# Linear attention, mixture of experts and a second network on one core: two maxima taken in another way

## The chip, the core and the metric

The kernel runs on 1 core of a Trainium2 chip. The metric is the device time of one execution in microseconds (us). Engines are named as the profile names them: PE (matrix products; PEld is its weight load), DVE (VectorE), ACT (ScalarE), POOL (GpSimd) and SP (SyncE, which only issues transfers here). Each engine takes its instructions in program order; an instruction waits for the semaphores of those it needs.

## The reference

Three parts follow each other. The first is attention without a softmax over pairs of tokens: q is normalised over its 64 features, k over the tokens.

```
q_s = exp(q - max(q, axis=-1));  q_s = q_s / (sum(q_s, axis=-1) + 1e-9)
k_s = exp(k - max(k, axis=2));   k_s = k_s / (sum(k_s, axis=2) + 1e-9)
kv  = einsum('bhsd,bhse->bhde', k_s, v)
out = einsum('bhsd,bhde->bhse', q_s, kv)
```

There are 8 batches, 8 heads, 576 tokens and 64 features, in float32. The second part sends each token to one of 8 experts (512 to 1024 to 512, ReLU); the third is `max(x@w1, x@w2, x@w3) @ w_out` (512 to 768 to 512).

## The kernel before

A **unit** is half of a batch's heads, so there are 16 units, n = 0 to 15, n = 2 * batch + half. A unit's q and k lie in SBUF as tiles of 128 partitions by 4 heads by 5 rows by 64 features: each partition holds five rows (tokens) of each head. The steps of a unit are small functions: `k_max` (maximum over the five rows, on DVE), `k_tr` (PE turns it, DVE finishes the maximum and puts it on a diagonal, L238 and L241), `k_exp` (PE spreads it into PSUM, the matmul at L248; DVE subtracts, L251; ACT takes the exponential, L253), `q_max` (maximum over 64 features for 20 rows, DVE L221), `q_exp` (DVE subtracts the row's maximum, L228; ACT takes one exponential over 1280 elements, L229; for unit 1 POOL subtracts), `q_sum` and `q_norm` (DVE, L259 to L268), `kv_mm`, `kv_norm`, then for each of two pairs of heads `q_tr` (PE turns q, ACT copies it rounded, L327, or L324 in the first two batches), `q_lo` (DVE subtracts the rounded copy to get the rest, L335), `x_mm` (PE, L353), `x_lo` (DVE L371) and `logit_mm`.

Beside this, PE works through the experts' products in **slots**. One slot is a group of 12 products of 128x288 (L611 for the first layer, L629 for the second), and 32 slots make a batch. Each result leaves PSUM through ACT and DVE in the first layer (L616, L617), and through ACT (L634, first half) or DVE (L636, second half) in the second; four PSUM buffers serve them. Experts' weights are split into a rounded part (ACT L588) and a rest (POOL L595). Pieces of the last network's weights are turned from float64 to float32 meanwhile (ACT L682 and L684, DVE L677 to L694, POOL L685, L686 and L695). POOL also issues indirect transfers for the router (L489).

The order is fixed by tables of slots. `STEADY` gives, for units 4 to 15, the slot of each step counted from the unit's START (16 slots apart). So the front steps of unit n+1 are written in between the back steps of unit n: the second pair of heads of unit n has `q_tr` in its slot 15, `q_lo` in 16 and `x_mm` in 17, and `q_max` and `k_max` of unit n+1 stand at slot 12, its `q_exp` at 15, its `k_tr` at 16. Within a slot the group of products comes first, then the steps of the older unit. Units 2 and 3 have their own table (`EARLY`); units 0 and 1 and the front of unit 2 run before the first expert product, in the order of the list `first`. This is the start, about 50 us long, in which PE has little to do. Below, a **second-half place** is the stretch in which an even unit's slots 12 to 17 meet the second layer of the second half (evictions by DVE L636); there are six of them, about 70 us apart. At the six places of odd units evictions go through ACT L634.

Of the kernel before, what the change touches and what calls it, by code (L numbers as in the profile page):

```python
# [9 lines left out]
F32 = mybir.dt.float32  # L10
# [3 lines left out]
ACTF = mybir.ActivationFunctionType  # L14
# [20 lines left out]

# batches whose attention output comes from plain float32 products instead of three with split operands
NFULL = 2

# The order of the work beside the experts' matrix products, in slots of one group of 12 products; a unit is
# half of a batch's heads. STEADY: slots after a unit's START for the steps in FRONT, and those in BACK for  # L40
# each pair of heads; EARLY: the same for the first units, from the first slot on. LOAD: a unit's loads.
# ROUTE: the router's steps after START of a batch's second unit, for batch 0 and 1 from the first slot on.
# DEC: pieces of the float64 weights, after START of even units, of odd units and of the last one.
STEADY = ((-4, -1, -4, 0, 1, 3, 6, 6, 7, 8), (10, 10, 13, 14, 15), (15, 16, 17, 18, 19))
EARLY = {
# [11 lines left out]
def tile_linear_attention__then__moe(  # L57
# [21 lines left out]

# [1 line left out]
    const = ctx.enter_context(tc.tile_pool(name="const", bufs=1))  # L81
# [24 lines left out]

# [1 line left out]
    es_moe = ExitStack()  # L108
# [20 lines left out]

# [1 line left out]
    def setup():  # L131
# [40 lines left out]

# [1 line left out]
    units = {}  # L174
# [35 lines left out]
    def k_max(b, hb):  # L210
        u = units[b, hb]
        u["mx"] = sm.tile([128, 4, D], F32, tag="kmx", name="kmx")
        vec.tensor_reduce(
            out=u["mx"], in_=u["k"].rearrange("p h c d -> p h d c"), axis=AX.X, op=ALU.max
        )

    def q_max(b, hb):
        u = units[b, hb]
        qt = u["q"].rearrange("p h c d -> p (h c) d")
        m = sm.tile([128, 20, 1], F32, tag="qm", name="qm")  # L220
        vec.tensor_reduce(out=m[:, :, 0], in_=qt, axis=AX.X, op=ALU.max)  # L221
        u["qm"] = m

    def q_exp(b, hb):
        u = units[b, hb]
        qt = u["q"].rearrange("p h c d -> p (h c) d")
        eng = nc.gpsimd if (b, hb) == (0, 1) else vec
        eng.tensor_tensor(out=qt, in0=qt, in1=u["qm"].to_broadcast([128, 20, D]), op=ALU.subtract)  # L228
        act(out=qt, in_=qt, func=ACTF.Exp)  # L229

# [141 lines left out]

    # the logits with tokens as columns: column tile c of the array takes tokens 128 c on; the last 64 follow on tile 0
    def logit_mm(b, hb, pr):
# [17 lines left out]

# [1 line left out]
    def route_1(b):  # L394
# [60 lines left out]
    def route_4(b):  # L455
# [22 lines left out]
        )  # L478
        # the position of a token that leaves its batch's majority expert; BIG for the others
        pool.tensor_scalar(out=a, in0=a, scalar1=-float(BIG), scalar2=None, op0=ALU.add)  # L480
# [12 lines left out]

# [1 line left out]
    events = {}  # L495
# [27 lines left out]
    for n, s0 in START.items():  # L523
        b, hb = divmod(n, 2)
        if n in EARLY:
            t, s0 = EARLY[n], 0
        else:
            t = STEADY
        if n > 2:
            at(LOAD.get(n, START.get(n - 2, 0) + 9), load_unit, b, hb)  # L530
        for d, f in zip(t[0], FRONT):
            if d is not None:
                at(s0 + d, f, b, hb)
        for pr in range(2):
            for d, f in zip(t[1 + pr], BACK):
                at(s0 + d, f, b, hb, pr)
        if hb == 1:
            s0 = START[n]
            r1, r2 = (s0 + ROUTE[0], s0 + ROUTE[1]) if n > 3 else ROUTE1
            at(r1, logit_tr, b)  # L540
            at(r1, route_1, b)
            at(r2, route_2, b)
            at(r2 + 3, route_3, b)
            at(r2 + 4, route_4, b)
            for c in range(5):
                at(r2 + 5 + 2 * c, route_5, b, c)
# [4 lines left out]

# [1 line left out]
    raw_t = {}  # L553
# [98 lines left out]

# [1 line left out]
    dec = deque((i, j) for j in range(8) for i in range(4))  # L654
# [12 lines left out]
    def dec_bits():  # L667
        if not dec_r:
            return
        i, j, raw = dec_r.popleft()  # L670
        lo, hi = raw[:, :, 0], raw[:, :, 1]
        f = dc_p.tile([128, 384], I32, tag="df", name="df")
        p = dc_p.tile([128, 384], I32, tag="dp", name="dp")
        a2 = dc_p.tile([128, 384], F32, tag="da", name="da")
        r = dc_p.tile([128, 384], F32, tag="dr", bufs=2, name="dr")
        # sign, exponent less 896 and the upper 20 bits of the mantissa
        vec.tensor_scalar(out=f, in0=hi, scalar1=0x07FFFFFF, scalar2=3,  # L677
                          op0=ALU.bitwise_and, op1=ALU.logical_shift_left)
        vec.scalar_tensor_tensor(out=f, in0=hi, scalar=-0x40000000, in1=f,
                                 op0=ALU.bitwise_and, op1=ALU.bitwise_or)  # L680
        vec.tensor_scalar(out=p, in0=f, scalar1=-0x00800000, scalar2=None, op0=ALU.bitwise_and)
        act(out=a2, in_=hi.bitcast(F32), func=ACTF.Abs)  # L682
        # the lower 32 bits, added with one rounding
        act(out=r, in_=lo.bitcast(U32), func=ACTF.Copy, scale=2.0 ** -52)  # L684
        nc.gpsimd.tensor_tensor(out=r, in0=r, in1=p.bitcast(F32), op=ALU.mult)  # L685
        nc.gpsimd.tensor_tensor(out=r, in0=r, in1=f.bitcast(F32), op=ALU.add)  # L686
        dec_m.append((i, j, a2, r))

    def dec_store():
        if not dec_m:  # L690
            return
        i, j, a2, r = dec_m.popleft()
        # under float32's range, by the upper word (0x38100000 and on, read as a float): zero
        vec.tensor_scalar(out=a2, in0=a2, scalar1=1.125 * 2.0 ** -15, scalar2=None, op0=ALU.is_ge)  # L694
        nc.gpsimd.tensor_tensor(out=r, in0=a2, in1=r, op=ALU.mult)  # L695
        dma(out=w32_d[i][:, j], in_=r)
# [7 lines left out]

# [1 line left out]
    m_all = [t.rearrange("p j n -> (p j n)").rearrange("(k f) -> k f", f=F2) for t in w32_d[0:3]]  # L706
# [29 lines left out]

    # ================= program =================
    with tc.manual_schedule():
# [95 lines left out]

# [1 line left out]
        sl = {}  # L836

        def fx_table():
# [43 lines left out]
            vec.tensor_reduce(out=sf[:, 0:4], in_=pr, axis=AX.X, op=ALU.add)  # L882
            # start = valid * (start0 + SLOT * j)
            vec.tensor_scalar(out=sf[:, 4:5], in0=jc, scalar1=float(SLOT), scalar2=None, op0=ALU.mult)
            vec.scalar_tensor_tensor(
                out=sf[:, 2:3], in0=sf[:, 4:5], scalar=sf[:, 3:4], in1=sf[:, 2:3], op0=ALU.mult, op1=ALU.add
            )
            # static start = min(start + CAP * (1 - valid), CAP)
            vec.tensor_scalar(
# [3 lines left out]
            vec.tensor_scalar(out=sf[:, 3:4], in0=sf[:, 4:5], scalar1=float(CAP), scalar2=None, op0=ALU.min)  # L893
            # trips of the general loop: 0 where the static slots cover everything
            nsl = incl[:, w - 1:w]
# [55 lines left out]

        # half a piece of a minority expert's weights: 256 rows of 512 columns
        def fx_w(e_reg, i):
# [33 lines left out]

        # the tokens' upper and lower parts side by side: the first pass multiplies both with the
        # weights' upper part, the second the upper part with the weights' lower part
        def fx_mm(ps, x, ws, kh):  # L990
# [9 lines left out]

        # adds the two parts and turns tokens to columns
        def fx_sum(raw):
# [62 lines left out]

        # steps between the groups of the second network; one that leaves its sum open in PSUM comes
        # only where the next step follows before that bank is needed again
        fix = deque((f, False) for f in (fx_table, fx_gather, fx_soft, lambda: None, fx_tr))
# [12 lines left out]

        # chunks: (sources of y, N, list of (scale, writer))
        def chunk_l2(c, hs, part=0):
# [20 lines left out]

        # chunk B holds the last 64 tokens of each batch, in two parts; the second carries the packed tokens
        order = [(c, 0) for c in range(B)] + [(B, 0), (B, 1)]
# [113 lines left out]
```

## Time and profile before

| what | us |
|---|---|
| median of 3 runs | 1250.62 |
| runs, lowest to highest | 1249.36 to 1254.8 |
| profiled execution: span from first to last instruction | 1248.6 |
| PE busy in the span | 1193.2 (96%) |
| DVE busy | 647.8 (52%) |
| ACT busy | 447.0 (36%) |
| POOL busy | 380.4 (30%) |

Only the span of the profiled execution is on the page; its whole time is not listed beside it. It lies 0.8 us under the fastest run and 2.0 us under the median, so whatever lies around the span is small. "Busy" is the share in which an engine had an instruction in flight. An idle time has a releaser: the instruction whose semaphore came last. The granted clock of PE is 1.00 at 2.4 GHz and 0.50 at 1.2 GHz.

### The profile page before, as it was taken

The page shows a single profiled execution, that of the slowest core. Times are in us where ns is not written, and L with a number is a line of the kernel's source. Part 1 is how long each engine was busy: PE and PEld are TensorE (multiplying, and loading weights), DVE is VectorE, ACT ScalarE, POOL GpSimd, SP SyncE. Part 2 cuts the span into 40 slices and gives each one's busy share as a digit, 9 for nine tenths or more (in the row PEclk, how much of TensorE's full clock was granted, in tenths as well). Part 3 has the DMA queues.
Part 4 walks back from the last instruction along what each step waited for, and adds up shares of the span by engine and source line. Part 5 has one row for each costly group of instructions (what it writes and reads, how often), then busy time and mean ns, then how long its engine had stood idle before and what let it go on. Part 6 is the DMA issues. An engine that isn't in the chain of part 4 may idle for free. (4 is left out here: it accounts for less than half of the span.)

```text
span 1248.6 us, 19283 instructions
## 1 busy us (share of the span) xinstructions
PE 1193.2 (96%) x7518; PEld 1054.4 (84%) x7518; DVE 647.8 (52%) x1161; ACT 447.0 (36%) x864; POOL 380.4 (30%) x466
## 2 busy tenths in 40 slices
PE   4699999999999999999999999999999999999996
PEld 3598998989899898999888888888888888888995
DVE  7779787787878789534442414132331313232211
ACT  2463554546454554534331223122232213221211
POOL 1257767676776667772002000000000000000000
PEclk9799999999999999999999999999999999999998
DMA  6776555675665544353512121211222111210001
GB/s 167 183 198 175 166 176 159 175 214 148 202 202 164 170 128 148 123 188 99 169 35 79 36 67 52 83 44 34 85 68 76 46 56 51 51 51 1 35 17 24
DMA packets 141455, 135.68 MB, mean 109 GB/s; under 512 B 70045, under 2 KB 104637, under 8 KB 140336
## 3 DMA queue, kind: packets, MB, share of 16 engines
q1 hardware_dynamic: 139648, 134.01, 36.1%
q8 instruction: 61, 1.00, 0.3%
q0 software_dynamic: 1712, 0.39, 0.2%
q14 instruction: 34, 0.28, 0.1%
HBM read 106.99 MB, written 27.62 MB: 108 GB/s over the span
## 5 line engine op out<-in xcount | busy, mean ns | idle before, releaser
L813 PE MATMUL pm<-yh,wf 128*128 128x512 f32 (+2 forms) x2160 | 464.8, 375 | 0.0
L813 PEld LDWEIGHTS pm<-yh,wf 128*128 128x128 f32 x2160 | 385.9, 188 | 72.5
L629 PE MATMUL yp<-h,w 128*128 128x288 f32 x1536 | 226.3, 303 | 0.2 <-DVE h L617 0.2
L611 PE MATMUL hp<-xs,w 128*128 128x288 f32 x1536 | 218.9, 299 | 0.0
L629 PEld LDWEIGHTS yp<-h,w 128*128 128x128 f32 x1536 | 212.1, 192 | 3.6 <-DVE h L617 0.5
L611 PEld LDWEIGHTS hp<-xs,w 128*128 128x128 f32 x1536 | 208.1, 190 | 2.8 <-POOL w L595 0.2
L595 POOL TENSOR_TENSOR w<-stg,w 128x512 fp32r<-128x512 f32 x126 | 179.4, 1427 | 77.0 <-ACT w L588 74.9
L820 DVE TENSOR_TENSOR tm<-tm,pm 128x512 f32<-128x512 f32 (+2 forms) x60 | 38.6, 643 | 256.6 <-ACT tm L819 152.3
L1077 POOL DMA_INDIRECT out_dram<-oc,ftb x1 | 1.0, 983 | 548.4 <-ACTq L1149 548.4
L831 PE MATMUL op<-wo,hc 128*128 128x512 f32 (+1 forms) x666 | 152.8, 390 | 0.0
L831 PEld LDWEIGHTS op<-wo,hc 128*128 128x128 f32 (+1 forms) x666 | 124.5, 187 | 26.3
L819 ACT ACTIVATE tm<-pm 128x512 f32<-128x512 f32 (+2 forms) x60 | 33.7, 562 | 230.9 <-PE pm L813 230.2
L617 DVE SCALAR_TENSOR_TENSOR h<-hp,h 128x288 fp32r<-128x288 f32 x128 | 56.6, 451 | 58.8 <-ACT h L616 58.5
L616 ACT ACTIVATE h<-hp 128x288 fp32r<-128x288 f32 x128 | 52.2, 408 | 84.6 <-PE hp L611 84.2
L588 ACT ACTIVATE w<-stg 128x512 fp32r<-128x512 f32 x128 | 78.8, 621 | 0.0
L823 ACT ACTIVATE hc<-tm 128x512 fp32r<-128x512 f32 (+2 forms) x60 | 35.8, 597 | 93.9 <-DVE tm L821 93.9
L824 DVE TENSOR_TENSOR hc<-tm,hc 128x512 fp32r<-128x512 f32 (+2 forms) x60 | 38.9, 649 | 39.8 <-ACT hc L823 39.8
L833 ACT ACTIVATE oc<-op,tsrc 128x512 f32<-128x512 f32 x32 | 22.1, 689 | 101.9 <-PE op L831 101.9
L489 POOL DMA_INDIRECT tab_d<-tsrc,rpi x40 | 45.9, 1147 | 37.5 <-DMA tab_d<-tsrc,rpi 26.2
L685 POOL TENSOR_TENSOR dr<-dr,dp 128x384 f32<-128x384 f32 x32 | 32.5, 1015 | 53.2 <-ACT h L616 37.3
L228 DVE TENSOR_TENSOR q<-q,qm 128x1280 f32<-128x1280 f32 x15 | 42.7, 2849 | 0.0
L821 DVE TENSOR_TENSOR tm<-tm,pm 128x512 f32<-128x512 f32 (+2 forms) x60 | 38.6, 644 | 7.0 <-DVE tm L820 0.9
(219 smaller groups left out, 1179.1 us busy)
## 6 DMA issues: line engine op xcount, KB each, us to landing
stg<-in_moe_w_dram SPq DMA_DIRECT2D x31, 1024.0 KB, 5.7
fw<-in_moe_w_dram SPq DMA_DIRECT2D x24, 512.0 KB, 3.8
v<-in_v_dram SPq DMA_DIRECT2D x80, 128.0 KB, 4.8
draw<-in_moe_w_dram SPq DMA_DIRECT2D x24, 384.0 KB, 4.1
y_d<-y SPq DMA_DIRECT2D x32, 288.0 KB, 2.7
k<-in_k_dram SPq DMA_DIRECT2D x16, 512.0 KB, 5.2
q<-in_q_dram SPq DMA_DIRECT2D x16, 512.0 KB, 6.6
yr<-y_d SPq DMA_DIRECT2D x8, 1024.0 KB, 5.2
```

The costliest lines, as they stand in the source:

```text
L228: eng.tensor_tensor(out=qt, in0=qt, in1=u["qm"].to_broadcast([128, 20, D]), op=ALU.subtract)
L489: nc.gpsimd.indirect_dma_start(out=tab_d[:, :], out_offset=bass.IndirectOffsetOnAxis(ap=rt[b]["pi"][:, c:c + 1], axis=0), in_=tsrc[:, b, c ...
L588: act(out=t[:, 0], in_=src, func=ACTF.Copy)
L595: eng.tensor_tensor(out=t[:, 1], in0=src, in1=t[:, 0].bitcast(F32), op=ALU.subtract)
L611: mm(ps, w[:, a, kk], xp[b, kk][:, c, cs], start=(n == 0), stop=(n == 11))
L616: act(out=h[:, 0, cs], in_=ps, func=ACTF.Relu)
L617: vec.scalar_tensor_tensor(out=h[:, 1, cs], in0=ps, scalar=0.0, in1=h[:, 0, cs].bitcast(F32), op0=ALU.max, op1=ALU.subtract,)
L629: mm(ps, w[:, a, f], ht[f][:, c, cs], start=(n == 0), stop=(n == 11))
L813: mm(pp[m][:, 0:n], wf[f][:, a, m, kk], ys[kk][:, c, 0:n], start=(kk == 0 and i == 0), stop=(kk == 3 and i == 2))
L820: vec.tensor_tensor(out=tv, in0=tv, in1=pp[1][:, 0:n], op=ALU.max)
L824: vec.tensor_tensor(out=h[:, 1, 0:n], in0=tv, in1=h[:, 0, 0:n].bitcast(F32), op=ALU.subtract)
L831: mm(ps[0:m], hs[f][:, a, 128 * t:128 * t + m], wo[f][:, c], start=(i == 0), stop=(i == 17))
```

## The change

`k_max` was one reduction over five rows on DVE; it becomes four maxima of two operands each, the first of rows 0 and 1, then the running maximum with rows 2, 3 and 4. `q_max` gets a second instruction that changes the sign of the 20 maxima. `q_exp` loses its subtraction; ACT takes 20 exponentials of 64 elements each, with the negated maximum of the row as bias. In the steady units the 20 come in four pieces of five, one piece in each of four slots, from slot -2 on (before: all at slot -1). Unit 1's subtraction on POOL goes too. Line numbers after the change are 2 higher from `k_tr` on and 5 higher from the experts on. The rest of the diff deletes comments.

```diff
-STEADY = ((-4, -1, -4, 0, 1, 3, 6, 6, 7, 8), (10, 10, 13, 14, 15), (15, 16, 17, 18, 19))
+STEADY = ((-4, -2, -4, 0, 1, 3, 6, 6, 7, 8), (10, 10, 13, 14, 15), (15, 16, 17, 18, 19))
...
-        u["mx"] = sm.tile([128, 4, D], F32, tag="kmx", name="kmx")
-        vec.tensor_reduce(
-            out=u["mx"], in_=u["k"].rearrange("p h c d -> p h d c"), axis=AX.X, op=ALU.max
-        )
+        kt = u["k"]
+        mx = u["mx"] = sm.tile([128, 4, D], F32, tag="kmx", name="kmx")
+        vec.tensor_tensor(out=mx, in0=kt[:, :, 0], in1=kt[:, :, 1], op=ALU.max)
+        for c in range(2, 5):
+            vec.tensor_tensor(out=mx, in0=mx, in1=kt[:, :, c], op=ALU.max)
...
         vec.tensor_reduce(out=m[:, :, 0], in_=qt, axis=AX.X, op=ALU.max)
+        vec.tensor_scalar(out=m, in0=m, scalar1=-1.0, scalar2=None, op0=ALU.mult)
         u["qm"] = m
...
-    def q_exp(b, hb):
+    def q_exp(b, hb, i=None):
         u = units[b, hb]
         qt = u["q"].rearrange("p h c d -> p (h c) d")
-        eng = nc.gpsimd if (b, hb) == (0, 1) else vec
-        eng.tensor_tensor(out=qt, in0=qt, in1=u["qm"].to_broadcast([128, 20, D]), op=ALU.subtract)
-        act(out=qt, in_=qt, func=ACTF.Exp)
+        for r in range(20) if i is None else range(5 * i, 5 * i + 5):
+            act(out=qt[:, r], in_=qt[:, r], func=ACTF.Exp, bias=u["qm"][:, r])
...
-            if d is not None:
+            if f is q_exp and d is not None and n not in EARLY:
+                for i in range(4):
+                    at(s0 + d + i, f, b, hb, i)
+            elif d is not None:
                 at(s0 + d, f, b, hb)
```

DVE at the first second-half place, before: `q_max` and `k_max` of unit 5 (L221, L213) stand ahead of the back steps of unit 4, with the subtraction of `q_exp` (L228) ahead of unit 4's last `q_lo` (L335).

```order
144 L221 TENSOR_REDUCE qm<-q 128x20
145 L213 TENSOR_REDUCE kmx<-k 128x256
146 L694 TENSOR_SCALAR da<-da 128x384
147 L636 TENSOR_TENSOR y<-yp,y 128x288 x2
148 L371 TENSOR_TENSOR xs<-xr,xs 128x576
149 L636 TENSOR_TENSOR y<-yp,y 128x288
150 L228 TENSOR_TENSOR q<-q,qm 128x1280
151 L636 TENSOR_TENSOR y<-yp,y 128x288
152 L335 TENSOR_TENSOR qTs<-qT,qTs 128x576
```

DVE at the same place, after (L214 and L216 are the four maxima, L337 is the `q_lo` that was L335):

```order
150 L222 TENSOR_REDUCE qm<-q 128x20
151 L223 TENSOR_SCALAR qm<-qm 128x20
152 L214 TENSOR_TENSOR kmx<-k 128x256
153 L216 TENSOR_TENSOR kmx<-kmx,k 128x256 x3
154 L699 TENSOR_SCALAR da<-da 128x384
155 L641 TENSOR_TENSOR y<-yp,y 128x288 x2
156 L373 TENSOR_TENSOR xs<-xr,xs 128x576
157 L641 TENSOR_TENSOR y<-yp,y 128x288 x2
158 L337 TENSOR_TENSOR qTs<-qT,qTs 128x576
```

Nothing changed its place; the subtraction of 1280 elements is gone from the queue ahead of the `q_lo`, and five instructions stand where one stood behind `q_max`.

ACT from the program's start, before: two exponentials of k, then two of q, then the copies of `q_tr`.

```order
1 L253 ACT_TABLE_LOAD
2 L253 ACTIVATE ke<-k 128x4x5x64 x2
3 L229 ACTIVATE q<-q 128x1280 x2
4 L324 ACTIVATE qTf<-qT 128x576 x2
5 L357 ACTIVATE xr<-xT_327 128x288
```

ACT at the same place, after:

```order
1 L255 ACT_TABLE_LOAD
2 L255 ACTIVATE ke<-k 128x4x5x64 x2
3 L231 ACTIVATE q<-q,qm 128x64 x40
4 L326 ACTIVATE qTf<-qT 128x576 x2
5 L359 ACTIVATE xr<-xT_371 128x288
```

Forty instructions stand where two stood, ahead of the same copies.

## Rows read from the trace of the kernel before

**Rows 1.** Windows: busy us of each engine (instructions), PE's granted clock, DMA share, GB/s.
```profile
0.00:60.00 60.00, 33.76 (x258) 24.90 (x259) 45.82 (x89) 21.77 (x37) 11.01 (x25) 0.89 0.71 173
...
120.00:520.00 400.00, 382.79 (x3182) 363.54 (x3182) 324.35 (x566) 204.85 (x416) 282.31 (x314) 0.98 0.57 170
```

**Rows 2.** Waits of PE from 120 to 520 us: total us, times, longest.
```profile
PE xT L353 <- DVE qTs L335: 14.2, 6, 2.7
PE kB L248 <- DVE dg L241: 2.8, 6, 0.5
```

**Rows 3.** Timeline of PE at the first second-half place: start, us, instruction, idle before.
```profile
125.53 1.06 PE L353 MATMUL xT<-qTs,kvs 128*128 128x288 f32 x6 [2.68 <-DVE qTs L335]
```

**Rows 4.** Timeline of DVE at the same place.
```profile
115.39 2.52 DVE L213 TENSOR_REDUCE kmx<-k 128x256 f32<-128x1280 f32 x1
...
118.30 0.81 DVE L636 TENSOR_TENSOR y<-yp,y 128x288 f32<-128x288 f32 x2
119.03 0.83 DVE L371 TENSOR_TENSOR xs<-xr,xs 128x576 fp32r<-128x576 f32 x1
...
120.15 4.30 DVE L228 TENSOR_TENSOR q<-q,qm 128x1280 f32<-128x1280 f32 x1
...
124.73 0.74 DVE L335 TENSOR_TENSOR qTs<-qT,qTs 128x576 fp32r<-128x576 f32 x1
```

**Rows 5.** Timeline of POOL at the same place.
```profile
115.88 1.31 POOL L595 TENSOR_TENSOR w<-stg,w 128x512 fp32r<-128x512 f32 x1
117.13 1.03 POOL L685 TENSOR_TENSOR dr<-dr,dp 128x384 f32<-128x384 f32 x1
118.24 1.00 POOL L686 TENSOR_TENSOR dr<-dr,df 128x384 f32<-128x384 f32 x1
119.40 1.40 POOL L489 DMA_INDIRECT tab_d<-tsrc,rpi  x1 [0.16 <-PE qT L321]
120.83 1.30 POOL L595 TENSOR_TENSOR w<-stg,w 128x512 fp32r<-128x512 f32 x1
```

**Rows 6.** Windows around second-half places, columns as in Rows 1.
```profile
126.60:130.00 3.40, 2.90 (x10) 2.75 (x11) 2.20 (x4) 1.48 (x3) 1.04 (x2) 0.50 0.35 135
194.90:198.30 3.40, 1.79 (x10) 1.53 (x11) 2.87 (x8) 2.96 (x4) 2.20 (x2) 0.99 0.95 288
...
409.90:413.30 3.40, 3.40 (x16) 3.31 (x15) 1.55 (x2) 1.92 (x3) 2.01 (x2) 0.50 0.12 38
474.70:478.10 3.40, 1.69 (x14) 1.46 (x12) 3.40 (x3) 0.45 (x1) 2.54 (x3) 1.00 0.73 273
```

**Rows 7.** Timeline: a 256-element DVE instruction with two SBUF inputs.
```profile
142.09 0.41 DVE L313 TENSOR_TENSOR kvs<-kvraw,kvs 128x256 fp32r<-128x256 f32 x1
```

**Rows 8.** Groups of ACT by shape: busy us, mean ns of one, idle before.
```profile
L588 ACT ACTIVATE w<-stg 128x512 fp32r<-128x512 f32 x128 | 78.8, 621 | 0.0
...
L819 ACT ACTIVATE tm<-pm 128x512 f32<-128x512 f32 x48 | 28.6, 597 | 195.5 <-PE pm L813 194.8
...
L833 ACT ACTIVATE oc<-op,tsrc 128x512 f32<-128x512 f32 x32 | 22.1, 689 | 101.9 <-PE op L831 101.9
...
L384 ACT ACTIVATE lgt<-lgT 128x128 f32<-128x128 f32 x8 | 2.2, 278 | 0.6 <-PE lgT L381 0.6
```

**Rows 9.** Timeline of the start and of the first slots, all engines.
```profile
5.49 2.31 DVE L213 TENSOR_REDUCE kmx<-k 128x256 f32<-128x1280 f32 x1 [2.89 <-DMA k<-in_k_dram]
...
17.84 1.27 ACT L253 ACTIVATE ke<-k 128x1280 f32<-128x1280 f32 x1 [3.32 <-DVE k L251]
...
25.81 1.49 DVE L259 TENSOR_REDUCE qs<-q 128x20 f32<-128x1280 f32 x1
...
43.92 1.27 ACT L229 ACTIVATE q<-q 128x1280 f32<-128x1280 f32 x1 [4.84 <-DVE q L228]
...
47.70 1.13 ACT L588 ACTIVATE w<-stg 128x512 fp32r<-128x512 f32 x2
...
64.09 1.28 ACT L229 ACTIVATE q<-q 128x1280 f32<-128x1280 f32 x1
```

## The prediction

> **What bounds the kernel now.** I read the windows first. From 120 to 520 us PE is busy 382.8 of 400 us, and the first 60 us are the only other stretch with much idle time: 33.8 of 60 [rows 1]. So PE's own work sets the time, and an edit on DVE, ACT or POOL counts only where it shortens one of PE's waits or adds one. The list of waits for the same 400 us explains the 17.2 us of idle time: 14.2 us in six waits of x_mm for DVE's L335, and 2.8 us in six waits of at most 0.5 for L241 [rows 2]. Six is the number of second-half places.
>
> The timeline of one such place shows why DVE is late. PE wanted L335's result at 125.53 - 2.68 = 122.85 [rows 3]. DVE gave it at 124.73 + 0.74 = 125.47, since L228 stood ahead of it for 4.30 us [rows 4]. The same 1280 elements take 1.49 in the one-operand L259 [rows 9], so L228 stood still for some 2.8 us. In that time POOL ended its L489, and then ran L595 and one more product [rows 5]. A DVE instruction that reads two operands from SBUF thus gives way to POOL. The one-operand L213 does not: it ran beside L595 and L685 in 2.52 us [rows 4, 5], and alone in 2.31 [rows 9].
>
> The wait has a second price. Behind five of these places PE's granted clock falls to 0.50, the lower of its two levels: first at 126.60 with PE busy 2.90 of 3.40 us, last at 409.90 with 3.40 [rows 6]. At half clock half of that is lost, some 1.6 us each, 8.0 in all. The stretch ahead of such a fall had PE busy 1.79 us or less of 3.40; at the sixth place it was 1.69 and no fall followed [rows 6].
>
> **The change part by part.** *The subtraction goes.* At the six places L228's 4.30 us leave the queue ahead of L335. Elsewhere it was covered already, as PE waits at no other place in the steady part.
>
> *Four maxima for one reduction.* No row has this operation on 256 elements; the nearest is L313 at 0.41 [rows 7]. Each needs the one before it, so I put one at 0.45 and four at 1.8 us. At the start, where POOL has nothing to do, that is 0.5 under L213's 2.31, twice in a row. At a second-half place POOL works without a pause. I follow the first place by hand [rows 4, 5]. The sign change (bounded by 0 and the 0.41 of L313; 0.2 taken) and the first maximum end near 116.1. POOL's L595 then has its turn to 117.3, as it waits while DVE's next maximum still needs the last one's result. With 0.3 for a maximum that waits ready and 0.1 less for a POOL product that does, the second maximum ends at 117.6, L685 at 118.4, the third at 118.7, L686 at 119.6, the fourth at 119.9. L213 ended at 117.91, so `k_max` is 2.0 us later, not 0.7 earlier. L371 followed L213's end by 1.12 and now comes at 121.0. There POOL's L489, shifted to 119.75, ends after its 1.40 at 121.15, and L595 follows for 1.30. If L371 waits for L595 alone it ends about 0.6 behind it, at 123.1; two L636 (0.81) and L335 (0.74) end it at 124.65. That is 0.8 us before the 125.47 of before, with PE still waiting 1.8. If L371 is passed over for two products, as L228 was, it ends about 1.0 later and L335 comes at 125.6, no better than before. If POOL takes no turn among the maxima, L335 is done before 122.85 and the wait is gone. So a place gains between 0 and its whole wait (2.4 on average); I take 0.8, six times: **4.8 us**. [...] I take three of five, 3 x 1.6 = **4.8 us** (bounds 0 and 8.0).
>
> The Trainium skill ("SBUF — State Buffer", section "SBUF: two separate sides") calls the port pair that VectorE and GpSimd share an exclusive lock, held for a whole instruction by whichever starts first, and counts a VectorE instruction with two SBUF inputs among those that need it. The trace agrees with 4.30 against 1.49. By that rule all four maxima ask for the lock that the reduction did not need, and a place gains the 0.8 above; without it the six waits would go entirely.
>
> *Twenty exponentials for one.* The nearest rows are 278 ns for 128 elements, and 689 against 597 ns for the same shape with and without a scale taken from a tile [rows 8]. From 597 and 278 an element costs 0.83 ns, so 64 elements take 225; 92 for the operand from a tile and 24 for a source in SBUF (621 against 597) make 341. Two L588 back to back take 1.13, 0.11 under twice 621 [rows 8, 9], so one follows the other after 0.23 us, and twenty take D = 4.6. The bounds are 0.17 (a 128-element one without the operand, overlapped) and 0.37 (with it, not overlapped): D = 3.4 to 7.4.
>
> In the steady part the pieces of five take 1.2 us in each of four slots. ACT is busy 205 of 400 us there [rows 1], the four PSUM buffers leave its evictions some slots of slack, and L327 at slot 15 stands behind one piece only: nothing for PE. Without that cover each slot would add up to 1.2.
>
> At the start nothing covers them. Unit 1's exponential of k (17.84) comes 1.0 earlier by two `k_max` and 0.2 later by the sign change, so it ends at 18.3. Units 0 and 1 then take 2D on ACT, to 27.5, and unit 1's row sum L259, at 25.81 before, starts 1.7 later; the router follows by as much. Unit 2's exponential gets some of that back. It stood at 43.92 after 4.84 us of waiting for L228, which was queued on DVE behind the router [rows 9]; its twenty can start at 39.1 + 1.7 and end at 45.4, against 45.2. The start thus costs 3D - 13.6 us: **+0.2**, from -3.4 to +8.6. In slot 3 unit 3's twenty stand in one piece: from 64.09 they end at 68.7 instead of 65.4 [rows 9], and what is queued behind, evictions and the copy of `q_tr`, is up to 3.3 late. The buffers take most of it; I put **+0.5** (0 to 3.3).
>
> The Trainium skill ("VectorE: DVE Perf Modes", section "Rules for kernel authors") tells one to keep the number of chained VectorE instructions small, since each drains. With its figure for a fixed cost of 151 cycles, four of 256 elements would be an estimated 1.70 us and one of 1280 1.49, and the start would lose 0.4 where I count a gain of 1.0. The trace has 2.31 for that reduction, and I go by it.
>
> **Sum.** +0.2 + 0.5 - 4.8 - 4.8 = -8.9. Against the profiled execution's span, 1248.6, that is 1239.7; the median of the runs lies 2.0 above that span, so **1242** us.
>
> **Rivals.** *The wait stays as long as it was.* L371, or already the maxima, lose to POOL until it pauses, as L228 did; DVE then has fewer elements but as many turns to wait for. For it speaks that POOL's products stand 0.1 us apart or less; against it that POOL itself moves. Price: no gain at the places, +0.7 elsewhere: 1251.
>
> *The wait goes entirely.* POOL's products wait for the first maximum, or DVE gets its turns close together, and L335 is ready at 122.85. For it: only 2.7 us are missing, of L228's 4.30. Price: -14.2 - 2.8 - 8.0 + 0.7 = -24.3, so 1226.
>
> *Slower: ACT at the start.* If one exponential follows the other after 0.31 us or more (D from 6.2 on), the start costs 5.0 or more and slot 3 another 1.5 to 3.3. With no gain at the places that is 1257 to 1262, say 1259. For it: an operand from a tile may break the overlap, which no row shows for such instructions. Against it: the two L588 that stand close do overlap [rows 9].
>
> **How the numbers follow.** The forecast (0.38) has its own range from 1236 to 1248; the wait that stays has 0.27, the wait that goes 0.18, the slower start 0.17. A measurement of this kernel tells 0.5%, 6.3 us, from no change. Faster by more than that (under 1244.4): the case in which the wait goes and 0.27 of the forecast's 0.38, 0.45. Slower (over 1256.9): 0.17. The rest, 0.38, lies within. The range from 1228 to 1257 leaves out about a tenth at each end, half of the case at 1226 and most of that at 1259.
>
> **What would show it.** The list of PE's waits from 120 to 520 us decides: x_mm for L337 near 9 us in six waits bears out the forecast, 13 or more the first rival, under 3 the second. The timeline of DVE at a second-half place shows whether the four maxima lie apart with a POOL product between each two, from 115.5 to about 119.9 relative to before. The half-clock windows should be two. At the start, the twenty exponentials should take 4.6 us, and the first split of an expert's weights (47.70 before) should come within 1 us of that; 5 us later means the slower case. A wait of PE in the slots of ACT's pieces, for an eviction or a copy of q, would prove the cover wrong.

## The result and the profile after

The changed kernel takes 1258.55 us (median of 5 runs, 1255.79 to 1262.32) against 1249.82 for the kernel before: a ratio of 1.0067, interval 1.0044 to 1.0090. It is slower by 8.7 us in the medians (8.4 by the ratio), where 8.6 faster were forecast. The profiled execution has a span of 1256.8 us against 1248.6.

Windows of the kernel after, columns as in [rows 1]. (After the change `x_mm` is L355, `q_lo` L337, the diagonal L243 and its product L250, the split of an expert's weights L593 and L600, the exponentials L231, the maxima L214 and L216.)

```profile
0.00:60.00 60.00, 32.54 (x245) 22.82 (x246) 38.46 (x93) 32.25 (x92) 7.15 (x24) 0.77 0.65 164
...
120.00:520.00 400.00, 381.90 (x3155) 361.35 (x3154) 324.94 (x597) 240.23 (x616) 274.66 (x317) 0.97 0.58 170
```

PE's idle time from 120 to 520 us is 18.1 us, where it was 17.2 [rows 1]. What it waits for there shows that the idle time has moved more than grown:

```profile
PE xT L355 <- DVE qTs L337: 11.5, 6, 2.2
PE kB L250 <- DVE dg L243: 6.5, 10, 1.3
```

The six waits of `x_mm` shrank from 14.2 to 11.5 us [rows 2]; those for the diagonal grew from 2.8 to 6.5, and five of the ten stand at places of odd units (2.5 us), where PE waited once before, for 0.54 us at 302.41. DVE and POOL at the first second-half place answer to [rows 4, 5]; the last row of the first fence is PE's.

```profile
120.67 0.42 DVE L214 TENSOR_TENSOR kmx<-k 128x256 f32<-128x256 f32 x1
121.12 3.69 DVE L216 TENSOR_TENSOR kmx<-kmx,k 128x256 f32<-128x256 f32 x3
...
125.74 2.93 DVE L373 TENSOR_TENSOR xs<-xr,xs 128x576 fp32r<-128x576 f32 x1
...
129.32 0.74 DVE L337 TENSOR_TENSOR qTs<-qT,qTs 128x576 fp32r<-128x576 f32 x1
...
130.12 1.81 PE L355 MATMUL xT<-qTs,kvs 128*128 128x288 f32 x6 [2.17 <-DVE qTs L337]
```

```profile
120.94 1.30 POOL L600 TENSOR_TENSOR w<-stg,w 128x512 fp32r<-128x512 f32 x1
122.20 1.19 POOL L690 TENSOR_TENSOR dr<-dr,dp 128x384 f32<-128x384 f32 x1
123.47 1.06 POOL L691 TENSOR_TENSOR dr<-dr,df 128x384 f32<-128x384 f32 x1
124.69 1.07 POOL L491 DMA_INDIRECT tab_d<-tsrc,rpi  x1 [0.16 <-issue]
125.78 1.30 POOL L600 TENSOR_TENSOR w<-stg,w 128x512 fp32r<-128x512 f32 x1
127.03 1.01 POOL L700 TENSOR_TENSOR dr<-da,dr 128x384 f32<-128x384 f32 x1
```

The first maximum ran in 0.42 us. Each of the next three ended with one POOL product, so three took 3.69 us, where at the start, with POOL idle, they take 1.34. Then L373, which came as the indirect transfer L491 ended, stood through L600 and L700 and took 2.93 instead of 0.8. L228 is gone, and DVE arrives only half a microsecond sooner relative to PE. Behind all six places PE's clock falls to 0.50, its lower level, where it fell behind five [rows 6]. Two windows at the first place and one at the last (489.60), which did not fall before:

```profile
129.20:132.60 3.40, 2.46 (x9) 2.06 (x9) 2.93 (x6) 0.63 (x1) 2.28 (x2) 0.60 0.99 296
132.60:136.00 3.40, 3.40 (x24) 3.31 (x23) 2.58 (x3) 3.20 (x9) 1.81 (x2) 0.90 0.07 21
...
489.60:493.00 3.40, 3.40 (x22) 3.24 (x21) 2.06 (x3) 1.98 (x3) 2.69 (x3) 0.69 0.14 52
```

Ahead of 75 us two things cost time. In the start, PE waits 6.3 us for unit 0's q behind twenty exponentials (2.7 before), and stays at half clock longer, from 20.67 to 37.74 us. Two windows of the kernel after:

```profile
20.40:23.80 3.40, 0.00 (x0) 0.00 (x0) 1.31 (x1) 3.40 (x16) 0.00 (x0) 0.54 0.00 0
...
34.00:37.40 3.40, 3.40 (x19) 1.95 (x17) 0.64 (x1) 1.54 (x4) 0.00 (x0) 0.50 1.01 181
```

The kernel before is at half clock there too, though its windows say 1.00: its trace has no record of the clock ahead of 31.0 us, and the 0.89 of the first 60 us [rows 1] is too high. The products tell more. Four products of `x_mm` take 2.29 us at half clock and 1.24 at full clock. The first two rows are of the kernel before, the next two of the kernel after, the last two of e1, which is told below:

```profile
28.44 2.29 PE L349 MATMUL xT<-qTf,kvraw 128*128 128x288 f32 x4
31.51 1.24 PE L349 MATMUL xT<-qTf,kvraw 128*128 128x288 f32 x4
...
33.28 2.29 PE L351 MATMUL xT<-qTf,kvraw 128*128 128x288 f32 x4
37.62 1.28 PE L351 MATMUL xT<-qTf,kvraw 128*128 128x288 f32 x4
...
39.21 2.29 PE L350 MATMUL xT<-qTf,kvraw 128*128 128x288 f32 x4
42.20 1.67 PE L350 MATMUL xT<-qTf,kvraw 128*128 128x288 f32 x4
```

The clock was thus back at 31.0 us before, at 37.7 after and, by its own record, at 43.1 in e1. PE's first product on unit 0's q comes 1.1 us later than before and the router's count 3.8 later; in e1 the two are 2.7 and 7.2 later.

In slot 3, ACT runs unit 3's twenty in one piece; the eviction L621 comes behind them, DVE stands 3.82 us for it, and the diagonal that is queued behind is late for PE. Three rows of the timeline, of ACT, DVE and PE:

```profile
65.93 4.87 ACT L231 ACTIVATE q<-q,qm 128x64 f32<-128x64 f32 x20
...
71.13 0.46 DVE L622 SCALAR_TENSOR_TENSOR h<-hp,h 128x288 fp32r<-128x288 f32 x1 [3.82 <-ACT h L621]
...
73.40 0.67 PE L250 MATMUL kB<-dg,ones 128*128 128x256 f32 x2 [2.47 <-DVE dg L243]
```

A ledger puts a size on each stretch. PE runs the same 7518 products in the same order in every kernel here, so one and the same product can be found in two traces. The table gives how much later it starts than in the kernel before (us; the heads are its start there), and each kernel's median with its ratio to the kernel before. A row of the table is one execution: the traced one of e6 took 4.3 us more than its kernel's median, that of e9 3.4 and that of e3 2.5 more, the others are within 2.1. The experiments are told below.

| kernel | 62.0 | 75.1 | 115.1 | 520.1 | median | ratio (interval) |
|---|---|---|---|---|---|---|
| after | +1.9 | +4.6 | +5.1 | +8.4 | 1258.55 | 1.0067 (1.0044 to 1.0090) |
| e1 | +5.6 | +9.9 | +10.4 | +2.7 | 1250.68 | 0.9998 (0.9983 to 1.0012) |
| e2 | -0.9 | -0.9 | -0.9 | +9.5 | 1259.28 | 1.0067 (1.0050 to 1.0084) |
| e3 | +1.9 | +2.3 | +2.8 | +8.6 | 1256.33 | 1.0052 (1.0035 to 1.0069) |
| e4 | -1.0 | +3.3 | +3.8 | +8.0 | 1258.07 | 1.0052 (1.0035 to 1.0068) |
| e5 | -0.1 | +0.2 | +1.1 | -6.0 | 1243.30 | 0.9943 (0.9929 to 0.9957) |
| e6 | -1.4 | -1.1 | -0.3 | -7.2 | 1243.15 | 0.9939 (0.9925 to 0.9952) |
| e7 | -0.1 | -0.1 | +1.4 | +17.5 | 1265.43 | 1.0114 (1.0099 to 1.0129) |
| e8 | -1.6 | -1.2 | -1.0 | -3.9 | 1246.63 | 0.9965 (0.9951 to 0.9979) |
| e9 | +0.4 | +0.7 | +1.3 | +4.4 | 1252.96 | 1.0018 (1.0008 to 1.0027) |
| e10 | -0.2 | -0.2 | +0.0 | +19.4 | 1270.39 | 1.0145 (1.0123 to 1.0166) |
| e11 | -1.4 | -1.0 | -0.5 | +2.2 | 1254.06 | 1.0032 (1.0015 to 1.0048) |
| e12 | +0.2 | +0.5 | +4.3 | +0.1 | 1251.99 | 1.0021 (1.0002 to 1.0041) |

So of the loss, 1.9 us arise in the start, 2.7 in unit 3's piece (4.6 - 1.9) and 3.8 from 75 to 520 us (8.4 - 4.6). Split by place, the 3.8 are 0.5 from 75 to 115 us, 1.0 in the six stretches of second-half places (115 to 145 us, 180 to 215 and so on), 2.9 in the five of odd places between them, and -0.5 at the end.

### The profile page after: what moved, and what is told of

Read it like the earlier page. It is cut to its first block, busy times and chain, and to the rows that moved or that the text cites. A ratio compares the mean times of both kernels' runs of the same rounds, so it can differ in the third digit from the quotient of the medians.

```text
span 1256.8 us, 19633 instructions
## 1 busy us (share of the span) xinstructions
PE 1196.7 (95%) x7518; PEld 1055.1 (84%) x7518; DVE 639.8 (51%) x1210; ACT 502.5 (40%) x1168; POOL 371.2 (30%) x465
## 5 line engine op out<-in xcount | busy, mean ns | idle before, releaser
L600 POOL TENSOR_TENSOR w<-stg,w 128x512 fp32r<-128x512 f32 x126 | 174.2, 1387 | 102.6 <-ACT w L593 100.7
L825 DVE TENSOR_TENSOR tm<-tm,pm 128x512 f32<-128x512 f32 (+2 forms) x60 | 38.6, 644 | 256.5 <-ACT tm L824 151.7
L621 ACT ACTIVATE h<-hp 128x288 fp32r<-128x288 f32 x128 | 52.1, 407 | 82.9 <-PE hp L616 82.7
L231 ACT ACTIVATE q<-q,qm 128x64 f32<-128x64 f32 x320 | 81.4, 335 | 0.0
L593 ACT ACTIVATE w<-stg 128x512 fp32r<-128x512 f32 x128 | 79.1, 621 | 0.8 <-DMA stg<-in_moe_w_dram 0.7
L491 POOL DMA_INDIRECT tab_d<-tsrc,rpi x40 | 43.1, 1077 | 40.0 <-DMA tab_d<-tsrc,rpi 29.2
L373 DVE TENSOR_TENSOR xs<-xr,xs 128x576 fp32r<-128x576 f32 x32 | 40.8, 1278 | 14.3 <-ACT xs L365 12.4
```

Of the source, the lines that this page charges most:

```text
L231: act(out=qt[:, r], in_=qt[:, r], func=ACTF.Exp, bias=u["qm"][:, r])
L373: vec.tensor_tensor(out=t[:, 1], in0=xr, in1=t[:, 0].bitcast(F32), op=ALU.subtract)
L491: nc.gpsimd.indirect_dma_start(out=tab_d[:, :], out_offset=bass.IndirectOffsetOnAxis(ap=rt[b]["pi"][:, c:c + 1], axis=0), in_=tsrc[:, b, c ...
L593: act(out=t[:, 0], in_=src, func=ACTF.Copy)
L600: eng.tensor_tensor(out=t[:, 1], in0=src, in1=t[:, 0].bitcast(F32), op=ALU.subtract)
L621: act(out=h[:, 0, cs], in_=ps, func=ACTF.Relu)
```

## The experiments

Line numbers shift with each edit; the names of functions and tiles stay.

**e1: the reduction back.** In `k_max` of the kernel after:

```diff
-        vec.tensor_tensor(out=mx, in0=kt[:, :, 0], in1=kt[:, :, 1], op=ALU.max)
-        for c in range(2, 5):
-            vec.tensor_tensor(out=mx, in0=mx, in1=kt[:, :, c], op=ALU.max)
+        vec.tensor_reduce(out=u["mx"], in_=u["k"].rearrange("p h c d -> p h d c"), axis=AX.X, op=ALU.max)
```

> The changed kernel with k's maximum as one reduction again, all else of the change kept. My theory: at the second-half places the four maxima take turns with POOL and so took the place of the subtraction's wait; without them L337 is done before PE wants it. The x_mm waits of 120 to 520 us, 11.5 us in six, go under 2, the kB waits, 6.5 us in ten, go under 2, no half-clock stretch follows a place any more (six before), and the time is 20 to 26 us under the changed kernel's, about 1235. Rival A, the loss sits in the twenty exponentials and the start and the places wait for another reason: within 3 us of the changed kernel's 1258. Rival B, the reduction (2.5 us) is itself nearly as late as the maxima: x_mm waits of 6 to 9 us remain, half-clock stretches stay, 1250 to 1255.

It came 7.9 us under the changed kernel, not 20 to 26. From 120 to 520 us the `x_mm` waits are gone, as expected, and so are all half-clock stretches but one. Other waits, 14.6 us in all where the changed kernel has 18.0, stand in their place. PE's waits of e1, 120 to 520 us:

```profile
PE qT L321 <- DVE qn L269: 8.2, 6, 1.7
PE kB L249 <- DVE dg L242: 4.8, 5, 1.2
PE yp L633 <- DVE h L621: 1.6, 5, 0.3
```

My theory held for the place and failed for the time: it had nothing late behind L337. The ledger adds what I had not foreseen at all: with the reduction the start and unit 3 cost 9.9 us, more than with the maxima, and 7.7 are then won back from 115 to 520 us. These 7.7 are a difference of two larger numbers: the stretches of second-half places give 24.6 us, nearly what the prediction's second rival had for them, and the odd ones, into which the wait for `q_norm` falls, take 16.8.

**e2: the maxima alone.** The kernel before with the change's `k_max`.

> The kernel before with only the four maxima put in; its subtraction and single exponential stay. My theory: the maxima and the subtraction both take turns with POOL at the second-half places, so x_mm waits grow from 2.4 to about 4 us each, 10 us in all, and the time is 8 to 12 us over the kernel before. Rival, the maxima are cheap and only the exponentials cost: within 2 us of the kernel before, with x_mm waits near 14 us in six as there.

As the theory had it: 9 us slower. The ledger has the whole loss behind 115 us (10.4), and 0.9 gained in the start. PE's waits:

```profile
PE xT L354 <- DVE qTs L336: 23.1, 11, 3.8
```

**e3 and e4: the two early losses, one at a time.** e3 spreads unit 3's exponentials over slots 3 to 6; e4 leaves units 0 to 2 as before.

```diff
-            if f is q_exp and d is not None and n not in EARLY:     (e3)
+            if f is q_exp and d is not None:
+        if 2 * b + hb < 3:                                          (e4, in q_exp)
+            eng = nc.gpsimd if (b, hb) == (0, 1) else vec
+            eng.tensor_tensor(out=qt, in0=qt, in1=u["qm"].to_broadcast([128, 20, D]), op=ALU.subtract)
+            act(out=qt, in_=qt, func=ACTF.Exp)
+            return
```

> The changed kernel with unit 3's twenty exponentials also in four pieces of five, in slots 3 to 6. My theory: its twenty in one piece (4.9 us on ACT) held an eviction on ACT, DVE stood still behind it, and the diagonal of L243 and with it PE came 2.5 us late at 73 us; in pieces that wait of 60 to 120 us goes and the time is 2 to 3 us lower. Rival, the buffers hide the piece and the shift of 2.6 us has another cause: no change, and the wait of 2.5 us at L250 stays.

> The changed kernel with units 0 to 2, the start, computed as in the kernel before: subtraction on DVE (on POOL for unit 1) and one exponential over 1280 elements, no sign change; the maxima stay everywhere. My theory: the half-clock stretch of 20.7 to 37.7 us, which the kernel before did not have, came from the 6.3 us that PE waited behind the exponentials for unit 0's q; it goes, the first kB product of the experts' time (51.87) comes 2 to 4 us earlier, and the time is 2 to 4 us lower. Rival, twenty exponentials cost as much as subtraction and one exponential at the start: within 1 us, and the half-clock stretch stays.

Both do locally much of what was expected: in e3 the 2.5 us wait at L250 is gone and PE is 2.3 us ahead of the changed kernel at 75 us; in e4 PE is 2.8 ahead at 62 us, and full clock is back at 30.4 us. Neither kept it. e4 lost 1.6 at once (its wait behind unit 3's piece is still 2.47, and half clock follows it), and by 520 us both stand within 0.4 of the changed kernel. Their medians are 2.2 and 0.5 lower, which the intervals do not separate from it. As the traced execution of e3 was 2.5 us over its median, it stays open whether the others of e3 kept its gain. In e3 the `x_mm` waits are the same 11.5 us, and those for the diagonal 8.7 instead of 6.5.

**e5: only the exponentials of units 3 to 15.** e1, e3 and e4 together.

> The changed kernel with k's maximum as one reduction, with units 0 to 2 as before (subtraction and one exponential) and with unit 3's exponentials in four pieces: only the twenty exponentials of units 3 to 15 are left of the change. e1 lost 9.9 us against the kernel before up to 75 us and won 7.2 of them back up to 520. Theory A, these are local sums: at 75 us this kernel stands within 1 us of the kernel before, and the 7.2 us of the places come off: about 1243. Rival B, lead is given back (e3 led the changed kernel by 2.3 us at 75 us and by nothing at the end): it ends where e1 did, 1249 to 1251, with longer waits at the places than e1's 8.2 us for q_norm and 4.8 us for L242's diagonal.

1243.30, theory A to the microsecond. The exponentials as biased pieces are worth 7 us where they stand in steady slots. PE's waits are those of e1, and DVE's and POOL's rows behind the first second-half place show what they come from:

```profile
PE qT L327 <- DVE qn L275: 8.9, 6, 1.8
PE kB L255 <- DVE dg L248: 4.7, 5, 1.1
```

```profile
131.22 1.76 DVE L267 TENSOR_SCALAR qs<-qs 128x20 f32<-128x20 f32 x1
...
133.54 2.29 DVE L689 SCALAR_TENSOR_TENSOR df<-draw,df 128x384 int32<-128x384 int32 x1
...
141.64 2.21 DVE L275 TENSOR_TENSOR qn<-q,qs 128x1280 f32<-128x1280 f32 x1
```

```profile
130.61 0.99 POOL L496 DMA_INDIRECT tab_d<-tsrc,rpi  x1 [3.16 <-DMA tab_d<-tsrc,rpi]
131.63 1.30 POOL L605 TENSOR_TENSOR w<-stg,w 128x512 fp32r<-128x512 f32 x1
133.10 0.99 POOL L496 DMA_INDIRECT tab_d<-tsrc,rpi  x1 [0.17 <-issue]
134.11 1.30 POOL L605 TENSOR_TENSOR w<-stg,w 128x512 fp32r<-128x512 f32 x1
```

L267 works on 20 elements and ends with the first L605; L689 ends with the second. They need 0.2 and 0.6 alone. As L228 did, these two stand behind an indirect transfer and what POOL runs after it, and `q_norm` is what comes late.

**e6: maxima where POOL is idle.** e5 with the four maxima in units 0 to 2 only.

> As e5, but units 0 to 2 take k's maximum by four pairwise maxima, where POOL has nothing to do; from unit 3 on it is the reduction. Theory: four maxima cost 1.7 us where the reduction costs 2.3 when nothing shares SBUF with them, so the first split of an expert's weights comes 1.1 us earlier than in the kernel before (as it did in e2), and the time is 1 us under e5's. Rival, the start's lead is lost later: within 0.5 us of e5.

The ledger has 1.3 us gained at 62 us and 1.2 still there at 520; the medians differ by 0.15, with intervals as wide as the gain. The theory is neither shown nor refuted by the time.

**e7: the subtraction later.** The kernel before, with one line changed.

```diff
-STEADY = ((-4, -1, -4, 0, 1, 3, 6, 6, 7, 8), (10, 10, 13, 14, 15), (15, 16, 17, 18, 19))
+STEADY = ((-4, 2, -4, 0, 1, 5, 6, 6, 7, 8), (10, 10, 13, 14, 15), (15, 16, 17, 18, 19))
```

> The kernel before with one step moved: q's subtraction and exponential at a unit's slot 2 in place of -1, and its row sum at slot 5 in place of 3. The subtraction still takes turns with POOL, but no longer ahead of the step that PE waits for. Theory A, its position ahead of L335 was the whole price: the x_mm waits of 14.2 us and the half-clock stretches go, and the time is 15 to 22 us under the kernel before, 1228 to 1235. Rival B, the queue of DVE has no room and the wait moves to the next late step (as e1's moved to q_norm): waits of 6 to 14 us for q_norm or the row sum, 1240 to 1251.

Neither: 1265.43, 15 us slower. The `x_mm` waits are gone, but `q_norm` is late at every unit, 3 us behind the second-half places and 1.3 behind the odd ones:

```profile
PE qT L320 <- DVE qn L268: 24.9, 11, 3.1
```

The place at which the subtraction stood was thus cheaper than this one, which moves the exponential and the row sum along with it. To take the work off DVE, as the exponentials' bias does, is worth 7 us; this move cost 15.

**e8, e9, e12: three ways to take away e5's wait for q_norm.** e8 (on e6) sets `q_norm` to slot 5; e9 (on e5) moves the router's indirect transfers; e12 (on e5) moves one float64 piece.

```diff
-STEADY = ((-4, -2, -4, 0, 1, 3, 6, 6, 7, 8), ...                    (e8)
+STEADY = ((-4, -2, -4, 0, 1, 3, 6, 6, 7, 5), ...
-                at(r2 + 5 + 2 * c, route_5, b, c)                    (e9)
+                at(r2 + 18 + 2 * c, route_5, b, c)
-DEC = ((5, 10), (3, 8, 11), (18, 26))                                (e12)
+DEC = ((1, 5, 10), (8, 11), (18, 26))
```

> As e6, with q_norm of the steady units at slot 5 in place of 8, so that it stands on DVE ahead of kv_norm, kv_lo and the products of the float64 pieces in between. Theory: the 8.2 us in six waits of q_tr for L269, which took the place of the x_mm waits in e1, go, and so does the one half-clock stretch behind them: 7 to 10 us under e6. Rival, the three slots do not matter since DVE is late as a whole: the wait appears at kv_lo, at an eviction or at the diagonal, and the time stays within 3 us of e6.

> As e5, with the router's five indirect transfers per batch (L496) moved from a batch's slots 25 to 33 to slots 38 to 46, away from the second-half place and from what follows it. In e5 the wait had moved to q_norm: DVE's L267 took 1.76 us and L689 2.29, each while POOL ended an indirect transfer and ran the product behind it. Theory: without the transfers these two take 0.2 and 0.6, q_norm is 3 us earlier, the 8.9 us in six waits go, and the time is 6 to 11 us under e5's 1243. Rival A, POOL's products alone keep DVE as late: qT waits stay over 6 us and the time within 3 us of e5. Rival B, the transfers do the same harm at their new place: waits of L248's diagonal or of x_mm at the odd places grow by as much.

> As e5, with one of the three float64 pieces of an odd unit (slot 3, just behind its second-half place) moved to slot 1 of the even unit, so that L687, L689 and L691 leave DVE's queue ahead of q_norm. In e5 these three took 2.95 us there at 133.2 and L704 1.1 at 136.9, of which some 2 us were spent behind POOL. Theory: q_norm comes at least 2 us earlier, the 8.9 us in six waits of q_tr go, nothing else is that close, and the time is 6 to 10 us under e5's 1243. Rival, as in e8 and e9 another step is next: waits of the same size at evictions, at L248 or at L343, and the time stays within 3 us of e5.

All three did away with the wait for `q_norm` (8.9 us in e5; none, 1.1 and 0.2 here), and all three are slower than e5, by 3 to 10 us. The largest wait from 120 to 520 us of each, in this order, e8, e9 and e12:

```profile
PE yp L646 <- DVE h L634: 9.0, 6, 1.8
```

```profile
PE cnt L423 <- DVE roh L417: 9.7, 5, 3.0
```

```profile
PE cnt L423 <- DVE roh L417: 9.6, 5, 2.0
```

The rivals hold in kind, as another step is next, an eviction in e8, the router's count in e9 and e12; in time they do not, as all three lose more than 3 us, and the step that came next in e9 was in neither of its rivals. In e12 the waits of 120 to 520 us sum to 11.5 us, less than e5's 15, but 3.8 us are lost from 75 to 115 us, and three half-clock stretches are back where e5 had one.

**e10: the transfers out of the way of L228.** The kernel before with e9's line.

> The kernel before with only that move: the five indirect transfers of a batch (L489) from slots 25 to 33 to slots 38 to 46. Theory: at a second-half place L228 stood still 2.8 us, since POOL's L489 and the product behind it went first; now it waits for one product, about 1.3 us, so the six x_mm waits shrink from 2.4 to about 1 us each, and the time falls by 6 to 12 us, to about 1241. Rival, L228 waits until POOL pauses, whatever POOL runs: x_mm waits stay over 2 us and the time within 3 us of the kernel before.

At the place itself the theory holds to the row. The fence has DVE at the first place; before, L228 took 4.30 [rows 4], and the wait of `x_mm` 2.68:

```profile
120.12 2.21 DVE L228 TENSOR_TENSOR q<-q,qm 128x1280 f32<-128x1280 f32 x1
...
123.73 2.03 DVE L241 TENSOR_SCALAR dg<-ident,m 128x128 f32<-128x128 f32 x2
```

`x_mm` now waits 0.2 to 0.5 there. But L241 behind it takes 2.03 beside POOL, where two alone take 0.48, and at the odd places, where the transfers now stand, `x_mm` waits 2.0 to 2.3. The time is 18 (by the ratio) to 20 us (by the medians) up. In the ledger the stretches of second-half places give back 11.0 us and those of the odd ones take 30.8, 6.5 to 7.4 in four of the five: behind each of these four PE waits for `x_mm` and the diagonal, and a stretch of half clock of 6.8 us follows, where the kernel before has none.

**e11: the maxima on e5.**

> As e5, with the four maxima in place of the reduction in all units: the changed kernel without its cost at the start and in unit 3. Theory, the parts add: exponentials in the steady units give 7 (e5), maxima take 9 (e2), so 2 us over the kernel before, about 1252, 6 under the changed kernel. Rival, the lead is given back at the places as e3's was: 1256 to 1258, with x_mm waits of 11 us and diagonals' waits over 8.

1254.06: 2 over the sum of the parts, and under the rival. From 75 to 520 us the maxima cost 9.4 us here (+3.2 against -6.2 of e5), 10.4 in e2 and 11.0 between e1 and the changed kernel. Three pairs of kernels, with and without the exponentials, agree on some 10 us; the medians of the first two pairs differ by 10.8 and 8.9.

## Why the prediction was wrong

**The second-half places (forecast -9.6 with the clock; measured +3.8 from 75 to 520 us).** This step failed. The replay of DVE's queue had the order of DVE and POOL right, up to L373 being passed over by two products, which the prediction had as "no better than before". From there it went to "a place gains between 0 and its whole wait", of which "I take 0.8". The 0.8 was a middle between two ends, where the replay pointed to the lower one; the gain was 0.5 at the first place and 0.35 to 0.46 at the others. In the terms of the sum, the waits of `x_mm` gave 2.7 us and not 4.8, the clock took some 1.6 where 4.8 were to come back, and the diagonal, which the sum had at nothing, took 3.7. Three things were missing. The clock: "three of five" falls were to end, a term that no run shows; with waits shorter by 0.35 to 0.5 us none ended, and a sixth came, while e1 and e5, in which the waits are gone, have one fall left. The step behind: L243 takes its turns with POOL too, so the wait for the diagonal at second-half places went from 2.3 to 4.1 us. And "PE waits at no other place in the steady part" was a misreading: of the six waits for L241 only five stand at second-half places, and one at an odd place (302.41, 0.54 us). At the odd places the changed kernel has five such waits, 2.5 us, and those stretches make 2.9 of the loss.

The two halves of the change have opposite signs there. The exponentials give about 6 us from 75 to 520 (e5 in the ledger) and the maxima take about 10 (e2, e11). The prediction had weighed them in one replay and could not see this. Its rule of the lock, from the Trainium skill ("SBUF — State Buffer", section "SBUF: two separate sides"), is borne out by 0.42 us for a maximum ahead of POOL's work against 1.2 for one that takes turns with it; the step failed in the sums drawn from it.

**The start (forecast +0.2, measured +1.9).** D was 4.9 (20 exponentials in 4.87), near the 4.6 estimated, and with it the sum 3D - 13.6 gives +1.0. Unit 1's row sum started 1.45 us later, near the 1.7 forecast. What failed is "the router follows by as much": it came 3.8 later, since PE ran the products in between at half clock until 37.7 us, where full clock was back at 31.0 before. Some of this came back later, as forecast, since unit 2's exponentials no longer wait for L228. It is the exponentials that lengthen the half clock: the eleven kernels here without them in the start are back at full clock by 32.6 us, the three with them (the changed kernel, e1, e3) at 37.7 or later. With the reduction the start costs 5.6 us (e1), so the maxima hid 3.7 of it, four times what they gain there alone (0.9 in e2). Of the 3.7, 1.6 are there at PE's first product on unit 0's q, and 1.8 arise up to the router's count, where e1 is at half clock until 43.1 us.

**Unit 3 in one piece (forecast +0.5, measured +2.7).** "The buffers take most of it" was wrong: the buffers hold PE's results, but DVE's queue stood behind one eviction, and the diagonal in it was late. e3 removes that wait.

**The steady pieces (forecast 0).** Right: no wait for an eviction or a copy of q on ACT shows among PE's from 120 to 520 us in the changed kernel.

**The rivals.** The slower one gave 1259, and the time came out there by luck, not by its mechanism: it needed D of 6.2 or more. "The wait stays" was nearest in the places, and L373 did stand until POOL paused, as it says; its 1251 was too low by the start, unit 3 and the diagonal. "The wait goes entirely" is what e1 and e5 do at `x_mm`, and there 1226 was too low, since waits for `q_norm` and the diagonal take its place.

That removed waits come back elsewhere is shown in e1, e5, e8, e9, e10 and e12. That DVE and POOL, which take turns, have no slack left in the steady part is how I read them together; a run with less work on both was not made. Of the 3.8 us from 75 to 520, idle time (0.9 more) and the sixth fall of the clock (some 1.6, as each of the others) account for about 2.5; the rest is not assigned.

## What to carry to other kernels

Where two engines take turns, count the turns an edit asks for, not its elements: four short instructions with two SBUF inputs cost 10 us in places where one longer reduction lost 0.2 us beside the other engine. Before pricing a wait that goes, ask which step of the same queue is next, with how much slack. And test the parts of a change apart: here one half gained 7 us and the other lost 9, and the better kernel (e5, 0.9943, 0.9929 to 0.9957) keeps the first and drops the second.

## What the runs showed of the hardware

- Four DVE instructions that stood when an indirect transfer of POOL ended, or came just then, stood on until POOL's next gap, of 0.16 us or more: L228 through L595 and the product after it (4.30 us, against 2.21 in e10 without the transfer), L373 through L600 and L700 (2.93, in the kernel after), L267 and L689 through one L605 each (1.76 and 2.29, in e5). Among POOL products alone, the maxima had every second turn.
- Not only two operands count. L267, one operand of 20 elements, took 1.76 us beside POOL (0.18 alone), and the sign change L223 took 0.54 on average over 16. The reductions hardly waited: L213 took 2.52 [rows 4] against 2.31 alone.
- The reduction over five strided rows takes 2.31 us and that over 64 neighbours 1.47, for the same 1280 elements. Four maxima of 256 take 1.80 with POOL idle.
- For a stretch of the start PE runs at half clock in every kernel here, also where the trace has no record of it and the windows print 1.00: the products of `x_mm` that follow each other are 0.48 us apart at half clock and 0.24 at full.
- An exponential over 64 elements with a bias from a tile takes 0.335 us, and one follows another after 0.24.
